# A block's left rows in one tile: per-step loads of 8 rows replaced by a shifted read of zero-padded probabilities

## The chip, the cores and the metric

The kernel runs on one core of one Trainium2 chip. The metric is the device time of one execution in microseconds (us). Engines: PE is TensorE, with PEld for its weight loads; DVE is VectorE, ACT is ScalarE, POOL is GpSimd, SP is SyncE, which here only issues DMAs. Each engine works through its own instructions in program order; a DMA instruction hands a transfer to the 16 DMA engines and lands later.

## The reference, cut to what matters

The output is x + A(xn) + B(xn), with xn the normalised x (2048 rows of 512), and all gradients of it for a given grad_out. B is a two-layer network with a squared ReLU. A is attention with a recurrent memory, 32 heads of 128:

```python
for s in range(n_seg):                          # 64 segments of 32 rows
    xs = x[:, s * seg_len:(s + 1) * seg_len, :].copy()
    h = jnp.concatenate([mem, xs], axis=1)      # 8 memory rows + 32 rows
    q, k, v = (jnp.einsum('btd,dhe->bhte', h, W) for W in (Wq, Wk, Wv))
    scores = jnp.where(mask, jnp.einsum('bhqe,bhke->bhqk', q, k) * scale, -1e9)
    p = _softmax(scores, axis=-1)
    o = jnp.einsum('bhqk,bhke->bhqe', p, v)
    o = jnp.einsum('bhte,hed->btd', o, Wo)
    mem = o[:, :M, :].copy()                    # M = 8: the next segment's memory
```

(q, k, v are three lines in the original.) Each segment needs the memory that the one before it left, so the forward pass is a chain of 64 steps; the gradient is a chain of 64 steps in the other direction.

## The kernel before, in words

**Stages.** From the start to about 255 us of the span: normalisation, B and its gradients, and products that don't depend on the chain. 255 to 1125 us: the forward chain. 1125 to 1385: gradients that don't depend on the backward chain, mixed with weight gradients of B. 1385 to 2335: the backward chain. 2335 to the end: weight gradients of A.

**Main rows and left rows.** Of a step's 40 rows, 32 are its main rows: 8 memory rows and the last 24 of the segment. The first 8 rows of the segment are its left rows; their q, k and v don't depend on the chain and are computed ahead, for many segments at once, and kept in the DRAM tensor S_NL. Four steps make a block (index b, step j = 0 to 3 in it; the backward chain runs j = 3 first and j = 0 last), and a block has 4 x 8 = 32 left rows. Heads are held as 4 groups g of 8 heads k, group g on partitions 32g to 32g+31. The left rows' own attention is done per block (functions left and lback); a main step (functions fwd and bwd) needs the left rows only as 8 further keys, besides its 32 main rows, so it works on L = 40 columns in this order: main 0 to 31, left 32 to 39.

**A forward step** (fwd, line 866): projections of k, q, v; transposes; scores s0, s1 (two halves p of the heads); softmax (mx, sb, ex, su, rc, pm) into the tile E of 64 columns per head, of which the last 24 stay zero; tu (line 480), a DVE transpose of E in 32 x 32 blocks into ET, so that block 0 has the main keys on partitions and block 1 the left keys, on the first 8 of them; w (line 931), the product of probabilities and v by the helper outer (line 620): for each head a matmul over the 32 main rows, and one over the 8 rows of the tile f_vLs; then the output projection.

**f_vLs and b_kLs.** f_vLs holds a step's 8 left rows of v, at partitions 32g to 32g+7, loaded for each step by left_of_step (line 639), four DMAs of 16 KB on SP. In the backward chain b_kLs holds the 8 left rows of k in the same way; there is one buffer of it, so its load for the next step waits until the last product that reads it is done. VL, a block's 32 left rows of v, is loaded besides for the left rows' own attention (line 746).

**A backward step** (bwd, line 1311): o0mm, o1mm, the projection of the incoming gradient (line 422); scores; d1 to d4, the gradient of the scores into gS (line 579); tu, its transposition into gST; vp, kp, qp (helper outer), the gradients of v, k and q, in PSUM tiles, where kp and qp of one half p lie in the same banks; the evictions ve, vl, ke, kl, qe into G4 and others (vea is the first of v; keb0 the first of k); vg, kg, qg, the projections back (line 490); ra, rb, ta, tb, H, the sum that is the next step's input. qp is, for each head, a matmul over the 32 rows of b_kN and one over the 8 rows of b_kLs; qp1, the second half, is the last reader of both. G4 holds a block's main gradients of v, k, q; when the block's last step is done, they are stored to S_GB (line 1238) in six DMAs of 512 KB on SP, named vo1, vo0, qo0, ko0, ko1, qo1. The first step of the next block writes its evictions into the same G4, so these wait for the stores.

**What sets the order.** Two strings written out by hand, F_ORDER and B_ORDER, name every operation in the order in which all engines are given it; each engine's instructions follow that order. A string has four parts, one for each step of a block; a name with n plus signs belongs to the step or block n later or earlier; names with L. are the per-block work. In B_ORDER before, the load of b_kLs is `ldk`, once per step; at the change of blocks SP's order is L.lq (load of b_gqL), vo1, L.qst (a store to S_GL), vo0, qo0, ko0, ko1, ldk, qo1, the load b_vl. POOL issues the loads b_P, b_qN, b_kN and others.

Of the kernel before, what the change touches and what calls it, by code (L numbers as in the profile page):

```python
# [8 lines left out]
ALU = mybir.AluOpType  # L9
# [3 lines left out]
P = 128  # L13
# [13 lines left out]
def kernel(  # L27
# [145 lines left out]
    def masks(pool, temp):  # L173
# [11 lines left out]
        for g in range(HG):  # L185
            sl = slice(32 * g, 32 * g + 32)

            keep(maskA[sl, :, M:SEG], [[0, KM], [-1, XS]], -M, 1)
            nc.gpsimd.memset(maskA[32 * g:32 * g + M, :, :], 0.0)

            keep(maskl1[sl, 0], [[-M, SPB], [0, M]], 0, 1)
            keep(maskl1[sl, 0], [[M, SPB], [0, M]], M - 1, -1)
            keep(maskl1[sl, 1], [[-M, SPB], [-1, M]], 0, 1)
            keep(maskl1[sl, 1], [[-M, SPB], [0, M]], 0, 1)
            keep(maskl1[sl, 1], [[M, SPB], [0, M]], M - 1, -1)
# [298 lines left out]

    C01, C23 = slice(0, 2), slice(2, 4)
# [67 lines left out]
    def ds_ops(o, p, n, sc, Pb, gS, sm):  # L563
# [14 lines left out]
        def d4():  # L578
            nc.vector.scalar_tensor_tensor(out=gS()[:, HALF[p], 0:n], in0=t[0][:], scalar=scale,  # L579
                                           in1=Pb()[:, HALF[p], :], op0=ALU.mult, op1=ALU.mult)  # L580
# [30 lines left out]
    def outer(pp, h, jobs, base=0):  # L611

        for k in range(4):
            for i, (c0, w, ends, m, N_, X) in enumerate(jobs):
                for g in range(HG):
                    o = pp[g // 2][:, g % 2, base + k * c0:base + k * c0 + w]
                    if ends:
                        o = o.rearrange("p (a n) -> p a n", a=2)[:, :, 0:M]
# [16 lines left out]

    def left_of_step(eng, dst, b, j, t):

        for g in range(HG):
            eng(dst[32 * g:32 * g + M], S_NL[b, 32 * g + M * j:32 * g + M * j + M, t, :])
# [14 lines left out]
    def play(order, n, steps, lefts, step, blk, done=None):  # L654
# [25 lines left out]
        "ta+++ Ha+++ L.u2 L.mx0+ L.t1 soV+++ tb+++ L.X2 Hb+++",  # L680
# [5 lines left out]
        "rb+++ L.oa0+ ta+++ Ha+++ tb+++ Hb+++",  # L686
# [4 lines left out]
        "tu1+++ w1+++ L.lq++ oa1+++ ob1+++ g0+++ g1+++ soN++ ra+++ rb+++ ta+++ Ha+++ tb+++ L.otr+ Hb+++",  # L691
# [4 lines left out]
        "ta+++ Ha+++ rb+++ tb+++ Hb+++ km+++ L.t3+ q0mm++++ L.E5+ k0mm++++ L.ra+ xa+++ k0ev++++ q1mm++++ k1mm++++ "  # L696
# [5 lines left out]
    with psum("fr", 4) as fr, psum("fpp", 1) as fpp, \  # L702
# [18 lines left out]
        def block(b):  # L721

            if b not in blk:
# [4 lines left out]
                          "VL": (fo, [P, GW], BF16), "vM": (fo, [P, GW], BF16), "EL": (fo, [P, KH, KW], BF16),  # L728
# [11 lines left out]
        def left(b):  # L740
# [5 lines left out]
            o["lv"] = lambda: dma(B_["VL"][:], S_NL[b][:, 2, :])  # L746
# [28 lines left out]
            for p in range(2):  # L775
                def S_(p=p):
                    ps["s%d" % p] = big("ps_scL")
                    scores(ps["s%d" % p], B_["qL"], ((B_["kM"], NL), (B_["kL"], NL)), p, maskL)
# [8 lines left out]
                def W_(p=p):  # L787
                    ps["w", p] = pair_of_banks()
                    outer(ps["w", p], p, ((32, 32, False, 32, B_["vM"], lambda k: st["ET%d" % p][:, k % 4, 0, :]),
                                          (32, 32, False, 32, B_["VL"], lambda k: st["ET%d" % p][:, k % 4, 1, :])))  # L790
# [75 lines left out]
        def fwd(s):  # L866
# [11 lines left out]
            def load(s1):  # L878

                b1, j1 = divmod(s1, SPB)  # L880
                t = fs.tile([P, GW], BF16, name="f_vLs", tag="vLs")
                left_of_step(dma, t[:], b1, j1, 2)
                vLs[s1] = t

            def ld():
                if s + 1 < NSEG:
                    load(s + 1)
            o["ld"] = ld

            def ld0():  # L890
                turned_rows(B_["kL"][:], 0, 1)
                load(0)
            o["ld0"] = ld0
            o["kl"] = lambda: nc.gpsimd.tensor_copy(T["kT"][:, :, :, SEG:L], B_["kL"][:, :, :, lc])
            o["km"] = lambda: nc.gpsimd.tensor_copy(B_["kM"][:, :, :, lc], T["kT"][:, :, :, 0:M])  # L895

            for t, u, n in ((1, 2, "k"), (0, 1, "q"), (2, 0, "v")):
                for p in range(2):
# [14 lines left out]
                    def Te(n=n, p=p):  # L913
                        ENGS["%s%dTe" % (n, p)](T[n + "T"][:, HALF[p], :, 0:SEG], kgr(ps[n, p]))
                    o["%s%dfl" % (n, p)] = fl_
                    o["%s%dTe" % (n, p)] = Te
            for p in range(2):
# [6 lines left out]
                def tu(p=p):  # L924
                    st["ET%d" % p] = fo.tile([P, 4, 2, 32], BF16, name="ET", tag="ET%d" % p)
                    turn(st["ET%d" % p], E, p)
# [34 lines left out]
        vLs = {}  # L961
# [27 lines left out]
    with sb("la", 2) as la, sb("ls", 2) as ls, sb("lo", 1) as lo_, sb("wg", 2) as wg, psum("lpp", 1) as lpp, psum("lr", 4) as lr:  # L989
# [9 lines left out]
        def lback(i_):  # L999
# [27 lines left out]
            for p in range(2):  # L1027
# [12 lines left out]
                def S_(p=p):  # L1040
                    ps["s", p] = big("ps_sc")
                    scores(ps["s", p], T["gOT"], ((T["vTM"], NL), (T["vTL"], NL)), p, None)
# [8 lines left out]
                def qp(p=p):  # L1051
                    ps["x", p] = [lpp.tile([P, 2, 512], F32, name="l_pp", tag="pp%d" % x) for x in range(2)]
                    outer(ps["x", p], p, ((32, 32, False, 32, T["kM"], lambda k: st[p][:, k % 4, 0, :]),
                                          (32, 32, False, 32, T["kL"], lambda k: st[p][:, k % 4, 1, :])))
# [623 lines left out]
```

## Time and profile before

| what | value |
|---|---|
| median of 3 runs | 2922.25 us (2919.82 to 2928.49) |
| the profiled execution | 2915.0 us |
| its span, first to last instruction | 2913.1 us |
| busy share of the span: PE, PEld, DVE, ACT, POOL | 93%, 50%, 44%, 34%, 23% |
| mean granted TensorE clock | 0.971 |
| DMA packets, bytes | 835429, 561.50 MB |
| loads f_vLs and b_kLs | 256 each, 16 KB each, on SP |
| SP's issue of one of them (min, median, max) | f_vLs 271, 300, 1311 ns; b_kLs 272, 296, 2118 ns |

How to read it: a row of a group is the code line, the engine, the operation, output<-input with partitions x elements, and the count; after the first bar the busy time in us and the mean duration of one in ns; after the second bar the idle time of that engine just before such instructions and what ended it. Four matmuls on four groups of 32 partitions run side by side, so the busy time of a group can be far below count times mean. "issue" is time in which the engine waited for nothing that the profile shows. A granted clock of 0.50 means that TensorE ran at half speed.

### The profile page before, as it was taken

The page shows a single profiled execution, that of the slowest core. Times are in us where ns is not written, and L with a number is a line of the kernel's source. Part 1 is how long each engine was busy: PE and PEld are TensorE (multiplying, and loading weights), DVE is VectorE, ACT ScalarE, POOL GpSimd, SP SyncE. Part 2 cuts the span into 40 slices and gives each one's busy share as a digit, 9 for nine tenths or more (in the row PEclk, how much of TensorE's full clock was granted, in tenths as well). Part 3 has the DMA queues.
Part 4 walks back from the last instruction along what each step waited for, and adds up shares of the span by engine and source line. Part 5 has one row for each costly group of instructions (what it writes and reads, how often), then busy time and mean ns, then how long its engine had stood idle before and what let it go on. Part 6 is the DMA issues. An engine that isn't in the chain of part 4 may idle for free.

```text
span 2913.1 us, 115280 instructions
## 1 busy us (share of the span) xinstructions
PE 2702.2 (93%) x51252; PEld 1450.9 (50%) x51252; DVE 1277.8 (44%) x3754; ACT 1001.7 (34%) x2330; POOL 660.6 (23%) x1278
## 2 busy tenths in 40 slices
PE   7997999999999887888898999999999999999999
PEld 3444555555555555355454554455555444444444
DVE  4533566666665654343454545454445401100000
ACT  2313444444444445232333333333333301111111
POOL 1000000000000001122333433343334324332221
PEclk9998999999999998998899999999999999999999
DMA  9766477667676668999666687677767799999993
GB/s 250 259 207 164 138 184 189 184 188 182 180 192 166 170 156 201 227 225 213 148 167 164 179 220 173 172 180 211 184 170 181 223 273 224 220 209 237 217 210 71
DMA packets 835429, 561.50 MB, mean 193 GB/s; under 512 B 642177, under 2 KB 727698, under 8 KB 833394
## 3 DMA queue, kind: packets, MB, share of 16 engines
q1 hardware_dynamic: 794018, 431.40, 64.6%
q0 software_dynamic: 40912, 122.73, 14.0%
q8 instruction: 402, 6.59, 0.9%
q14 instruction: 97, 0.79, 0.1%
HBM read 174.47 MB, written 234.11 MB: 140 GB/s over the span
## 4 chain that ended last, share of the span: by engine, by line
PE 42%; DMA 7%; issue 2%; DVE 1%; SPq 1%; POOL 0%; ACT 0%; ACTq 0%; DVEq 0%; POOLq 0%
PE ps_gw L1639 17%; PE ps_gR L490 11%; PE ps_proj L422 3%; PE b_pp L620 3%; PE ps_RL L1251 3%; DMA b_kLs<-S_NL 2%; PE b_T L525 1%; PE ps_tr L164 1%; DMA gn<-S_OL 1%; DMA b_qN<-S_A 1%; PE ps_R L490 1%; DMA S_GM<-b_GN 1%; PE b_pp L1383 1%; PE ps_sc L467 1%; DMA b_GN<-GT 0%
## 5 line engine op out<-in xcount | busy, mean ns | idle before, releaser
L1639 PE MATMUL ps_gw<-gn,HNc 128*128 128x512 bf16 x1920 | 416.8, 379 | 0.0
L1639 PEld LDWEIGHTS <-HNc 128*128 128x128 bf16 x1920 | 187.9, 98 | 223.6
L404 ACT CAST f_N<-ps_proj 128x512 bf16<-128x512 f32 x320 | 183.9, 581 | 199.4 <-PE ps_proj L422 192.6
L1572 ACT CAST wt<-ps_gw 128x512 bf16<-128x512 f32 x128 | 74.0, 588 | 451.3 <-PE ps_gw L1639 412.0
L422 PEld LDWEIGHTS <-X 128*32 128x32 bf16 x6144 | 152.6, 96 | 143.1 <-DVE X L534 21.9
L1555 DVE TENSOR_TENSOR gx<-ps_rows,gb 128x512 f32<-128x512 f32 x16 | 11.1, 692 | 426.4 <-PE ps_rows L1553 426.4
L895 POOL COPY kM<-f_kT 128x256 bf16<-128x256 bf16 x64 | 25.8, 403 | 736.0 <-DVE f_kT L407 562.2
L490 PE MATMUL ps_gR<-Wv,gv 128*32 128x512 bf16 x2048 | 145.0, 404 | 6.9 <-issue 6.9
L1639 PE MATMUL ps_gw<-GOc,gn 128*128 128x512 bf16 x640 | 141.0, 383 | 10.2 <-ACT wt L1572 8.7
L490 PE MATMUL ps_gR<-Wk,gk 128*32 128x512 bf16 (+1 forms) x2048 | 141.1, 387 | 1.3 <-ACT gk L404 0.8
L490 PE MATMUL ps_R<-Wo,OT 128*32 128x256 bf16 x4096 | 135.6, 289 | 1.1 <-DVE OT L407 1.1
L422 PE MATMUL ps_proj<-Wq,X 128*32 128x512 bf16 x2048 | 134.7, 380 | 0.1
L404 ACT CAST gk<-b_pp 128x256 bf16<-128x256 f32 x192 | 70.7, 379 | 184.0 <-PE b_pp L620 116.1
L422 PE MATMUL ps_proj<-Wk,X 128*32 128x512 bf16 x2048 | 130.9, 380 | 0.8
L422 PE MATMUL ps_proj<-Wv,X 128*32 128x512 bf16 x2048 | 131.3, 382 | 0.0
L404 ACT CAST gON<-ps_proj 128x512 bf16<-128x512 f32 x128 | 75.0, 586 | 157.4 <-PE ps_proj L422 157.4
L490 PE MATMUL ps_gR<-Wq,gq 128*32 128x512 bf16 (+1 forms) x2048 | 122.8, 348 | 6.8 <-issue 6.8
L422 PE MATMUL ps_proj<-Wo,GT 128*32 128x512 bf16 x2048 | 123.3, 382 | 3.7 <-DVE GT L1296 3.6
L1573 POOL DMA_DIRECT2D out_dram<-wt x120 | 65.0, 543 | 255.7 <-ACT wt L1572 241.0
L1332 POOL COPY PD<-b_P 32x320 bf16<-32x320 bf16 x256 | 115.3, 450 | 8.0
L490 PEld LDWEIGHTS <-OT 128*32 128x32 bf16 x4096 | 109.3, 102 | 9.9 <-DVE OT L407 1.3
L1327 POOL DMA_DIRECT2D b_P<-S_A x63 | 33.9, 538 | 349.9 <-DVE gS L579 115.6
(276 smaller groups left out, 5256.7 us busy)
## 6 DMA issues: line engine op xcount, KB each, us to landing
S_A<-f_N SPq DMA_DIRECT2D x64, 512.0 KB
out_dram<-wt POOLq DMA_DIRECT2D x134, 128.0 KB, 4.9
S_A<-f_N SPq DMA_DIRECT2D x64, 256.0 KB
S_GB<-gv SPq DMA_DIRECT2D x32, 512.0 KB
S_GB<-gq SPq DMA_DIRECT2D x32, 512.0 KB
S_GB<-gk SPq DMA_DIRECT2D x32, 512.0 KB
b_kN<-S_A POOLq DMA_DIRECT2D x63, 256.0 KB, 3.9
b_qN<-S_A POOLq DMA_DIRECT2D x63, 256.0 KB, 4.1
```

What stands on the lines that cost most here:

```text
L164: nc.tensor.transpose(ps_ap, in_ap, ident[base:base + k, base:base + k])
L404: nc.scalar.copy(out, in_)
L422: nc.tensor.matmul(o, lhsT=hT[:, dc, :], rhs=x, start=(dc == 0), stop=(dc == DC - 1), tile_position=(0, 32 * g))
L467: nc.tensor.matmul(sc3[32 * g:32 * g + 32, k, c:c + n], lhsT=qT[:, 4 * h + k, g, :], rhs=kT[:, 4 * h + k, g, :], start=(mask is None), sto ...
L490: nc.tensor.matmul(R[32 * g:32 * g + 32, 0:(cs.stop - cs.start) * P].rearrange("p (a b) -> p a b", b=P), lhsT=XT(k, g), rhs=x[:, cs, :], s ...
L620: nc.tensor.matmul(o, lhsT=N_[32 * g:32 * g + m, kk * P:(kk + 1) * P], rhs=X(kk)[32 * g:32 * g + m], start=(i == 0), stop=(i == len(jobs) ...
L1251: nc.tensor.matmul(ps["R", i][32 * g:32 * g + 32, :].rearrange("p (a b) -> p a b", b=P), lhsT=B_[n][:, k, g, :], rhs=W(g * KH + k), start= ...
L1327: q(tile_of("P", [P, KH, KW])[:], rows[:, 3 * GW:AC].rearrange("p (k n) -> p k n", k=KH))
L1332: nc.gpsimd.tensor_copy(PD[32 * g:32 * g + 32, g], C["P"][32 * g:32 * g + 32, :, 0:L])
L1572: nc.scalar.copy(wt[:], ps[:])
L1573: eng(dst, wt[:])
L1639: nc.tensor.matmul(ps[:], lhsT=l(rc), rhs=r(rc), start=(n == 0), stop=(n == RC_ALL - 1))
```

## The change

In both chains a step's columns are put in the order left 0 to 7, main 8 to 39, and the 40 columns stand at the right end of the 64 of E and gS: columns 0 to 23 are zero, 24 to 31 left, 32 to 63 main. The DVE transpose then reads two windows of 32 columns per head: one from column 24 - 8j on, one from column 32 on. In the first window of step j the 8 left columns land on partitions 8j to 8j+7, behind 8j zeros; the product over it takes the first 8 + 8j rows of a tile that holds all left rows of the block, VL forward and kNL backward, so that the rows of other steps meet zeros. left_of_step, f_vLs and b_kLs are gone.

The forward chain uses VL, which now has two buffers and is loaded at the end of the first part of F_ORDER, one part earlier than before. The backward chain loads kNL once per block, in two halves (ldk1, then ldk0, 128 KB each) into one buffer; in SP's order these come right behind the first projections of the block's first step: ldk1, vo1, L.qst, ldk0, vo0, qo0, ko0, ko1, qo1. The rest of B_ORDER and F_ORDER names the same operations in the same order as before; the cuts between the four parts of B_ORDER lie elsewhere. Masks, copies and evictions take the columns at their new places.

```diff
-    def turn(ET, E, h):
-        nc.vector.transpose(ET[:].rearrange("p k a q -> p (k a q)"),
-                            E[:, HALF[h], :].rearrange("p k n -> p (k n)"))
+    def turn(ET, E, h, j=None):
+        if j is None:
...
+        else:
+            x = E[:, HALF[h], XS - M * j:]
+            nc.vector.transpose(ET[:].rearrange("p k a q -> p (k a q)"),
+                                bass.AP(x.tensor, x.offset, [x.ap[0], [KW, 4], [M + M * j, 2], [1, SEG]]))
...
-            e.tensor_tensor(out=E()[:, HALF[p], 0:n], in0=st[p][:], in1=bc(ss[1], n), op=ALU.mult)
+            e.tensor_tensor(out=E()[:, HALF[p], KW - n:KW], in0=st[p][:], in1=bc(ss[1], n), op=ALU.mult)
...
-    def left_of_step(eng, dst, b, j, t):
-        for g in range(HG):
-            eng(dst[32 * g:32 * g + M], S_NL[b, 32 * g + M * j:32 * g + M * j + M, t, :])
...
-                          "VL": (fo, [P, GW], BF16), "vM": (fo, [P, GW], BF16), "EL": (fo, [P, KH, KW], BF16),
+                          "VL": (fs, [P, GW], BF16), "vM": (fo, [P, GW], BF16), "EL": (fo, [P, KH, KW], BF16),
...
-                    outer(ps["w", p], p, ((32, 32, False, 32, T["N"][:, 0], lambda k: st["ET%d" % p][:, k % 4, 0, :]),
-                                          (32, 32, False, M, vLs[s], lambda k: st["ET%d" % p][:, k % 4, 1, :])))
+                    outer(ps["w", p], p, ((32, 32, False, 32, T["N"][:, 0], lambda k: st["ET%d" % p][:, k % 4, 1, :]),
+                                          (32, 32, False, M + M * j, B_["VL"], lambda k: st["ET%d" % p][:, k % 4, 0, :])))
...
-        "o0mm++++ pb+++ o1mm++++ L.vo1+ L.qst o0ev++++ L.vo0+ xa+++ L.xt L.qo0+ o1ev++++ o0fl++++ xb+++ L.ra0+ "
+        "o0mm++++ pb+++ o1mm++++ ldk1+++ L.vo1+ L.qst o0ev++++ ldk0+++ L.vo0+ xa+++ L.xt L.qo0+ o1ev++++ o0fl++++ "
...
-            o["ldk"] = lambda: left_of_step(dma, tile_of("kLs", [P, GW])[:], b, j, 1)
+            for p in range(2):
+                o["ldk%d" % p] = lambda p=p: dma(B_["kNL"][:, HC[p]], S_NL[b][:, 1, HC[p]]) if j == SPB - 1 else None
...
-                                     (32, 32, False, M, C["kLs"], lambda k: st[p][:, k % 4, 1, :])), 4 * KW)
+                                     (32, 32, False, M + M * j, B_["kNL"], lambda k: st[p][:, k % 4, 0, :])), 4 * KW)
```

More of the change, by code (lines that the diff above doesn't have):

```diff
@@ L493, in gather @@
                                  tile_position=(0, 32 * g))
+    MAIN = slice(M, L)
     C01, C23 = slice(0, 2), slice(2, 4)
@@ L578, in d4 @@
         def d4():
-            nc.vector.scalar_tensor_tensor(out=gS()[:, HALF[p], 0:n], in0=t[0][:], scalar=scale,
+            nc.vector.scalar_tensor_tensor(out=gS()[:, HALF[p], KW - n:KW], in0=t[0][:], scalar=scale,
                                            in1=Pb()[:, HALF[p], :], op0=ALU.mult, op1=ALU.mult)
@@ L745, in left @@
             o["lq"] = lambda: turned_rows(B_["qL"][:], b, 0)
-            o["lv"] = lambda: dma(B_["VL"][:], S_NL[b][:, 2, :])
+            o["lv"] = lambda: dma(B_["VL"][:], S_NL[b][:, 2, :]) if b > 0 else None
             o["lm"] = lambda: memory_rows(B_["vM"], b, 0)
@@ L876, in fwd @@
             ps, st, o = {}, {}, {}
[L878 to L888, printed above, removed]
             def ld0():
                 turned_rows(B_["kL"][:], 0, 1)
-                load(0)
+                dma(B_["VL"][:], S_NL[0][:, 2, :])
             o["ld0"] = ld0
-            o["kl"] = lambda: nc.gpsimd.tensor_copy(T["kT"][:, :, :, SEG:L], B_["kL"][:, :, :, lc])
-            o["km"] = lambda: nc.gpsimd.tensor_copy(B_["kM"][:, :, :, lc], T["kT"][:, :, :, 0:M])
+            o["kl"] = lambda: nc.gpsimd.tensor_copy(T["kT"][:, :, :, 0:M], B_["kL"][:, :, :, lc])
+            o["km"] = lambda: nc.gpsimd.tensor_copy(B_["kM"][:, :, :, lc], T["kT"][:, :, :, M:2 * M])
             for t, u, n in ((1, 2, "k"), (0, 1, "q"), (2, 0, "v")):
@@ L913, in Te @@
                     def Te(n=n, p=p):
-                        ENGS["%s%dTe" % (n, p)](T[n + "T"][:, HALF[p], :, 0:SEG], kgr(ps[n, p]))
+                        ENGS["%s%dTe" % (n, p)](T[n + "T"][:, HALF[p], :, MAIN if n == "k" else slice(0, SEG)], kgr(ps[n, p]))
                     o["%s%dfl" % (n, p)] = fl_
@@ L1384, in vp @@
                                          start=True, stop=False, skip_group_check=True)
-                        nc.tensor.matmul(o.rearrange("p g (a n) -> p g a n", a=2)[:, :, :, 0:M],
+                        nc.tensor.matmul(o[:, :, 0:2 * M].rearrange("p g (a n) -> p g a n", a=2),
                                          lhsT=B_["gOL"][:, k * P:(k + 1) * P],
@@ L1411, in bwd @@
                         o[e] = lambda n=n, x=x, gs=gs, p=p, at=at, w=w, e=e: ENGS[e](
-                            G4[n][:, gs, HALF[p], j, :], two_of(pp(p), x, w, *at)[:, :, :, 0:SEG])
+                            G4[n][:, gs, HALF[p], j, :], two_of(pp(p), x, w, *at)[:, :, :, MAIN if n == "k" else slice(0, SEG)])
                         if n == "k":
@@ L1471 @@
             first["ldn"](dma)
-            first["ldk"]()
+            first["ldk0"]()
+            first["ldk1"]()
             ldk(NB - 1, dma)
             for s in range(1, NSEG):
-                for n in ("vtr", "vc", "ldp", "pb", "ldq", "ldn", "ldk"):
+                for n in ("vtr", "vc", "ldp", "pb", "ldq", "ldn", "ldk0", "ldk1"):
                     steps[NSEG - s][n] = steps[NSEG - 1 - s][n]
-            for n in ("vtr", "vc", "ldp", "pb", "ldq", "ldn", "ldk"):
+            for n in ("vtr", "vc", "ldp", "pb", "ldq", "ldn", "ldk0", "ldk1"):
                 steps[0][n] = lambda: None
```

68 lines of the change are left out of this document (34 added, 34 removed), and 61 rows, old and new, of tables (B_ORDER, F_ORDER).

## The prediction

> **What bounds the kernel now.** I read the busy time by stage first, then who waits for whom in the backward recurrence, then the groups by shape, then the timelines of block ends. The first view cuts the span at the stage borders; its columns are the time, the busy us of PE, PEld, DVE, ACT and POOL, the granted clock, the DMA share and GB/s. The two chains that the change touches:
>
> ```profile
> 255.00:1125.00 870.00, 819.35 (x20735) 476.66 (x20734) 537.54 (x1686) 413.61 (x937) 55.58 (x135) 0.97 0.66 173
> 1385.00:2335.00 950.00, 875.48 (x22824) 474.85 (x22822) 462.77 (x1452) 359.57 (x977) 362.89 (x700) 0.97 0.72 184
> ```
>
> TensorE is busy 94% and 92% of them, so only what stops TensorE, or slows its clock, is worth time: 51 us forward and 75 us backward stand idle. The second view lists PE's waits in the backward chain (us in total, times, longest):
>
> ```profile
> PE b_pp L620 <- issue: 14.7, 9, 2.5
> PE b_pp L620 <- DMA b_kLs<-S_NL: 14.5, 16, 4.8
> PE ps_gR L490 <- issue: 13.9, 10, 3.0
> PE b_pp L620 <- ACT gk L404: 6.0, 5, 1.6
> PE b_pp L620 <- DMA b_qN<-S_A: 4.8, 7, 1.0
> ```
>
> The load that the change removes, b_kLs, is the largest wait with a name. In the chain that ended last it has 2.1% (61 us), but that counts the load's whole time; PE stood for 14.5 us of it. The forward twin f_vLs is in no PE wait (PEld waited 2.5 us for it), and the forward waits are for ET (24.0 us).
>
> **What the removed waits are worth.** From the PE timeline I measured each backward step from its first projection matmul to that of the next. A block's four steps, in the order they run: first 17.0 us (mean of 15 blocks, 14.8 to 19.4), second and third about 13.1 and 12.7 in every block, last 15.9 (14.05 to 20.8). So all that can be won lies in the first and the last step. In the last step b_kLs is late where SP, which issues in order, stood behind a chain of transposes:
>
> ```profile
> 1546.63 0.20 PE L620 MATMUL b_pp<-gST,b_kN 32*128 32x32 bf16 x4
> 1551.60 0.91 PE L620 MATMUL b_pp<-gST,b_kLs 8*128 8x32 bf16 x4 [4.77 <-DMA b_kLs<-S_NL]
> ```
>
> PE stops 4.77 us between two halves of one product. Such waits in last steps are 4.77, 0.61, 0.30, 1.32, 0.59, 0.71, 1.49 and 0.99: 10.8 us. The six steps that have them took 20.8, 16.7, 14.15, 17.9, 18.0 and 15.6 us, where the five undisturbed ones took 14.05 to 14.3: 18.5 us over 14.1 each. The 7.7 us beyond the idle time are slow clock: it reads 0.50 from 1549 to 1555. After the change nothing of this block is loaded in the last step, so I count **-18.5 us**. The Trainium skill (TensorE: Matmul & The Clock Gate, What's actually happening) has the clock halve only after an idle window of about 3.4 us; by that only the 4.77 us wait costs clock and this term would be about -13. The rows differ: after 0.68, 1.65 and 0.66 us of waiting between 1978 and 1983 the clock was 0.50 until 1989. I keep the rows.
>
> In the first step the waits with b_kLs's name are only 0.35, 0.66, 0.58 and 1.13 us, and there something else ends as late. SP's timeline of one block end, then what ACT and PE waited for (idle time and releaser in brackets):
>
> ```profile
> 1966.24 0.35 SPq L1216 DMA_DIRECT2D b_gqL<-S_GQL  x1
> 1966.70 1.95 SPq L1238 DMA_DIRECT2D S_GB<-gv  x1
> 1968.69 0.42 SPq L1283 DMA_DIRECT2D S_GL<-gNat  x1
> 1969.17 1.15 SPq L1238 DMA_DIRECT2D S_GB<-gv  x1
> 1970.41 0.91 SPq L1238 DMA_DIRECT2D S_GB<-gq  x1
> 1971.37 3.45 SPq L1238 DMA_DIRECT2D S_GB<-gk  x2
> 1974.86 4.17 SPq L639 DMA_DIRECT2D b_kLs<-S_NL  x4
> ...
> 1981.66 0.37 ACT L404 CAST gk<-b_pp 128x256 bf16<-128x256 f32 x1 [2.73 <-DMA S_GB<-gk]
> ...
> 1982.94 0.81 PE L620 MATMUL b_pp<-gST,b_kLs 8*128 8x32 bf16 x4 [0.66 <-DMA b_kLs<-S_NL]
> ```
>
> Six stores of 512 KB go out; from 1970 to 1982 the 16 DMA engines are full (share about 1.0, 300 to 400 GB/s). The next step's gk eviction waits for the first gk store to have left G4, qp0 waits for that eviction (they share a PSUM bank), and b_kLs, queued behind all stores, lands 1 us later. Both end late together.
>
> **What the change moves there.** The block's kNL (two halves of 128 KB, one buffer) is loaded ahead of vo1 and vo0, the gv stores. Its buffer is read by qp1 of the block's last step, so SP now stands at ldk1 until that is done. Call its last matmul group's start Q: 1911.21, 1968.24, 2204.22 in three blocks; vo1 went out before it, at 1910.31, 1966.70, 2202.67. Behind the waiting ldk1 on SP are vo1, the S_GL store, ldk0, vo0, qo0, ko0, ko1. Where the two gv stores go back to back and ACT then waits for ko0, that wait ended 13.2, 13.8 and 14.2 us after vo1 (three blocks). New vo1: Q + 0.2 + 0.45 (one issue). ko0 has then landed at about Q + 0.65 + 13.7 = Q + 14.4; in the eight blocks where ACT waited for it, it ended 12.9 after Q on average. PE's first kLs group now comes 13.9 us after Q (mean of 15); then Q + 14.4 + 0.45 = 14.85: +0.95 a block, +14 us over 15. In the same stretch PE now stands some 20 us for "issue" (2.85 at 1567.23, 2.55 at 1803.51), which the longer wait partly covers; I take a quarter of that off: **+9.5 us**. kNL's 256 KB against the 64 KB of b_kLs would add 0.5 us a block at 380 GB/s, but the 256 KB b_gqL load, first of the burst today, goes 1 to 2 us earlier once the four b_kLs issues ahead of it are gone (1.3 to 1.7 us of SP); I set these equal.
>
> **Parts that cost nothing.**
>
> ```profile
> L620 PE MATMUL b_pp<-gST,b_kLs 8*128 8x32 bf16 x2048 | 54.5, 175 | 22.5 <-DMA b_kLs<-S_NL 14.5 <-issue 7.3
> L620 PE MATMUL b_pp<-gST,b_kN 32*128 32x32 bf16 x2048 | 51.8, 177 | 7.9 <-ACT gk L404 6.0 <-issue 1.4 <-ACT b_gkL L404 0.4
> L620 PEld LDWEIGHTS <-b_kLs 8*128 8x128 bf16 x2048 | 39.3, 92 | 27.4 <-DMA b_kLs<-S_NL 16.2 <-issue 7.8
> L620 PEld LDWEIGHTS <-b_kN 32*128 32x128 bf16 x2048 | 37.8, 91 | 48.3 <-issue 46.8 <-DMA b_kN<-S_A 1.3
> ```
>
> The contraction over 8, 16, 24 or 32 rows in place of 8: 8 rows take 175 and 92 ns, 32 rows 177 and 91. No cost, and the count stays. Forward, 256 loads of 16 KB (1.2 us of SP a step) go, and the block's VL comes up to a step earlier, in two buffers; PE waited for neither, so 0; if a VL is late, w0 waits, at most what b_kLs cost in last steps. At blocks 4, 8 and 12 VL is read right after the store of its last rows; w0 is more than half a step later and covers it. STREAM_TRANSPOSE (445 and 440 ns) reads four overlapping windows instead of 256 contiguous columns: no row shows that. Nearest are reductions: 344 ns for 192 strided elements, 299 for 160 contiguous, the same per element, so I take 0; below nothing is excluded, the count of elements is the same. If it doubled, the 26 forward waits for ET and 6 backward ones for gS would pay 0.44 each: +14. The moved columns in masks, copies and evictions keep shapes and counts: 0.
>
> **Sum.** -18.5 + 9.5 = -9 us on the profiled execution's 2915.0 (span 2913.1, 1.9 around it): 2906. The median of the runs shown is 7.25 above that execution: **2913 us**. About 0.3% (9 us) is what a measurement of this kernel can tell from no change.
>
> **Rivals.**
> *The gain stays whole.* Across the 15 first steps the time from Q to kLs does not follow how early vo0 went (14.0 or so for early and late ones), which speaks for a burst that may shift free of charge. Then -18.5, -2.7 for the waits in first steps, and up to -10 of "issue" as the burst meets a stopped PE: -21 to -31, 2891 to 2901.
> *The stores become the wait (slower).* ldk1 delays vo0 from Q - 1.0 (mean of 15) to Q + 2.2. Counted from vo0, ko0 landed 12.75 us later (mean of eight); with 0.5 us for kNL that is Q + 15.5, PE at Q + 15.9, +2 a block: +30. The three blocks whose vo0 went after Q have first steps of 17.65, 19.4 and 18.9 us against a mean of 17.0, which speaks for it. With slow clock after the longer waits (1.5 us in half of the blocks) +41; less 18.5: +11 to +23, 2933 to 2945. It decides from 1.2 us a block on (18.5/15). The Trainium skill (DMA: Bandwidth & Descriptors, Queues, rings and completion order) says that an engine takes descriptors in ring order, so what stands ahead of ko0 is moved first; the trace shows SP's stores landing so, b_kLs after ko0.
> *The shifted read is slow:* +14 on the sum, 2927.
> *b_kLs was never the end of a wait:* "issue" gaps fill it, 0, 2922.
>
> **Chances.** Forecast 0.42 (its own range 2900 to 2924: faster 0.24, same 0.18), whole gain 0.16 (faster), stores 0.30 (slower 0.28, same 0.02), slow read 0.05 (slower 0.04, same 0.01), nothing 0.07 (same 0.05, slower 0.02). Together faster 0.40, same 0.26, slower 0.34. The range takes the whole gain's far end and the stores with all their slow clock and 10 us of first-step waits more: 2891 to 2955.
>
> **What would show it.** Last steps of blocks all at 14.1 to 14.5 us: the -18.5. Time from Q to the first kNL group near 14.9, with ACT waiting for S_GB<-gk in nearly all blocks: the +9.5; at 16, the stores rival; at 13.9 or less, the whole gain. STREAM_TRANSPOSE near 445 ns and a forward stage of 870 us: the zeros. The prediction is wrong if the waits for VL or kNL themselves appear on PE, or if the forward stage moves by more than 5 us.

## The result and the profile after

The changed kernel takes 2932.07 us (median of 20 runs, 2915.5 to 2946.9) where the kernel before takes 2916.52 us (20 runs, 2898.5 to 2933.75): the ratio is 1.0057, 95% interval 1.0039 to 1.0075. In a second comparison it was 1.0073 (1.0040 to 1.0107). The range of the prediction holds the time, but the sign is wrong: 9 us faster was forecast and it is 16 to 20 us slower. Most runs of a kernel lie within 20 us of its median, single ones 30 us away, and the kernel before is at 2901.6 to 2907.9 us in the later comparisons. So below a kernel is compared only with the kernel before of the same comparison: by the ratio with its 95% interval, or by the difference of the two medians in us.

The profiled execution took 2933.0 us (span 2931.2). First the two chains by stage, in the columns of the view shown of before (time, busy us of PE, PEld, DVE, ACT, POOL, clock, DMA share, GB/s), then the five longest of PE's waits in the backward chain (us in total, times, longest; 1385 to 2355 us, since the chain ends later than before):

```profile
255.00:1125.00 870.00, 807.71 (x20632) 468.90 (x20674) 535.55 (x1681) 408.54 (x930) 55.59 (x135) 0.98 0.65 168
1385.00:2335.00 950.00, 864.39 (x22566) 467.01 (x22569) 455.65 (x1435) 355.30 (x968) 359.61 (x698) 0.96 0.73 177
```

```profile
PE b_pp L626 <- ACT b_gvL L404: 16.7, 7, 3.3
PE ps_gR L495 <- issue: 10.5, 13, 2.4
PE b_pp L1372 <- DMA b_gOL<-S_GOL: 10.0, 5, 4.6
PE b_pp L626 <- ACT gk L404: 8.3, 8, 1.6
PE b_pp L626 <- DMA b_qN<-S_A: 7.2, 4, 2.7
```

PE is busy 91% of the backward stage instead of 92%. The wait for b_kLs is gone, and no wait for b_kNL has come. In its place stand waits for the v evictions, for b_gOL and for b_qN, which were small or absent. All of those for the v evictions (b_gvL) and for b_gOL are in the first step of a block. One block end, SP first, then the two ACT evictions and the PE groups that waited (idle time and releaser in brackets):

```profile
2216.86 0.33 SPq L1202 DMA_DIRECT2D b_gqL<-S_GQL  x1
2217.86 0.33 SPq L1323 DMA_DIRECT2D b_kNL<-S_NL  x1
2218.24 1.07 SPq L1224 DMA_DIRECT2D S_GB<-gv  x1
2219.36 0.44 SPq L1269 DMA_DIRECT2D S_GL<-gNat  x1
2219.85 0.81 SPq L1323 DMA_DIRECT2D b_kNL<-S_NL  x1
2220.70 1.13 SPq L1224 DMA_DIRECT2D S_GB<-gv  x1
2221.93 0.56 SPq L1224 DMA_DIRECT2D S_GB<-gq  x1
2222.53 2.86 SPq L1224 DMA_DIRECT2D S_GB<-gk  x2
2225.48 1.90 SPq L1224 DMA_DIRECT2D S_GB<-gq  x1
2227.48 6.03 SPq L1327 DMA_TRANSPOSE b_vl<-S_A  x1
...
2229.31 0.59 ACT L404 CAST gv<-b_pp 128x512 bf16<-128x512 f32 x1 [3.91 <-DMA S_GB<-gv]
2233.34 0.37 ACT L404 CAST gk<-b_pp 128x256 bf16<-128x256 f32 x1 [2.62 <-DMA S_GB<-gk]
...
2230.60 0.38 PE L626 MATMUL b_pp<-gS,b_qN 32*128 32x40 bf16 x4 [2.70 <-DMA b_qN<-S_A]
2233.76 0.21 PE L626 MATMUL b_pp<-gST,b_kN 32*128 32x32 bf16 x2 [0.62 <-ACT gk L404]
```

Q is 2217.53 here. The first kNL load leaves right after it, as forecast, and all six stores behind it. ACT now waits for a gk store in 15 of 15 blocks (33.4 us; 8 blocks and 19.9 us before) and, which nothing forecast, for a gv store in 9 (33.5 us; 4 and 3.5 us before). Two more things are to be seen, and the runs below turn on them: no issue stands between the second gk store and the second gq store, where before had four (4.17 us in the block that the prediction shows), and b_vl follows at once.

The rows for the parts that were to cost nothing:

```profile
L485 DVE STREAM_TRANSPOSE ET<-E 128x256 bf16<-128x256 bf16 x128 | 57.0, 445 | 4.4
L485 DVE STREAM_TRANSPOSE gST<-gS 128x256 bf16<-128x256 bf16 x128 | 56.3, 440 | 2.2
L626 PE MATMUL b_pp<-gST,b_kNL 8*128 8x32 bf16 x512 | 11.9, 172 | 1.0 <-issue 0.8
L626 PE MATMUL b_pp<-gST,b_kNL 32*128 32x32 bf16 x512 | 11.2, 177 | 0.0
```

The backward steps, from the timelines (mean us; a step runs from its first gON eviction to that of the next). "gq" and "vl" say how long after the first gk store the second gq store and the load of b_vl left SP (mean of 15 blocks). Each row is one execution; the backward chain of the kernel before took 933.1 us in one and 924.4 in another, so a row tells 0.3 us a step at best.

| kernel | first | second | third | last | gq | vl |
|---|---|---|---|---|---|---|
| before | 16.98 | 13.12 | 13.12 | 15.90 | 8.1 | 9.0 |
| before, second execution | 17.08 | 13.06 | 13.05 | 15.43 | 8.0 | 8.9 |
| changed | 19.56 | 13.10 | 12.94 | 14.33 | 3.3 | 5.5 |
| changed, second execution | 18.99 | 13.05 | 12.87 | 14.19 | 3.0 | 4.8 |

Read alone, these traces say: 1.6 and 1.2 us won in each last step, 2.6 and 1.9 lost in each first one, the stores' rival as it was described. The runs show that this is not the whole of it.

### The profile page after: what moved, and what is told of

Same layout as the page of the kernel before. It is cut to its first block, busy times and chain, and to the rows that moved or that the text cites. A ratio compares the mean times of both kernels' runs of the same rounds, so it can differ in the third digit from the quotient of the medians.

```text
span 2931.2 us, 114549 instructions
## 1 busy us (share of the span) xinstructions
PE 2691.9 (92%) x51115; PEld 1444.8 (49%) x51252; DVE 1276.8 (44%) x3754; ACT 1002.0 (34%) x2330; POOL 659.3 (22%) x1278
## 3 DMA queue, kind: packets, MB, share of 16 engines
q0 software_dynamic: 40912, 122.73, 14.3%
q8 instruction: 402, 6.59, 1.0%
## 4 chain that ended last, share of the span: by engine, by line
PE 71%; DMA 13%; SPq 6%; DVE 4%; issue 3%; ACT 2%; POOL 1%; another core or an unknown queue 0%; ACTq 0%; DVEq 0%; POOLq 0%
PE ps_gw L1627 15%; PE ps_proj L422 14%; PE ps_gR L495 11%; PE ps_R L495 4%; DMA S_GB<-gk 3%; PE b_pp L626 3%; PE ps_tr L164 3%; PE ps_RL L1237 2%; SPq L1072 2%; PE ps_L L380 2%; PE ps_sc L467 2%; PE ps_B L341 2%; PE f_T L531 2%; PE f_pp L626 2%; PE ps_gxb L350 1%
## 5 line engine op out<-in xcount | busy, mean ns | idle before, releaser
L495 PE MATMUL ps_gR<-Wv,gv 128*32 128x512 bf16 x2048 | 151.8, 419 | 1.3 <-issue 1.2
L495 PE MATMUL ps_R<-Wo,OT 128*32 128x256 bf16 x4096 | 128.1, 279 | 1.1 <-DVE OT L407 1.1
```

The source lines that it names most:

```text
L495: nc.tensor.matmul(R[32 * g:32 * g + 32, 0:(cs.stop - cs.start) * P].rearrange("p (a b) -> p a b", b=P), lhsT=XT(k, g), rhs=x[:, cs, :], s ...
```

## Experiments

**1. The order, the place, the forward half.** Theory W was the rival of the prediction: SP stands at the kNL load, so all stores leave later. Theory V blames the bytes of that load, theory U the shifted reads, the deeper contraction or the moved columns.

*order_only*: the kernel before with `ldk+++` taken from behind `L.ko1+` and put ahead of `L.vo1+`.

> The kernel before, with one edit: the load of the step's 8 left rows of k (64 KB, b_kLs) goes to the place in the order that the change gives kNL, ahead of the stores of the finished block, in all first steps of a block; tiles, shifted reads and the loads of the other steps are as before. Theory W (SP stands at the load until the block's last query product has started its last group, and all six stores leave later): first store about 2.8 us later than before (from Q - 2.1 to Q + 0.7), first kLs group from Q + 13.7 to Q + 15.7, first steps of blocks from 17.0 to about 19.5 us, so +30 to +39 us: 2946 to 2955 beside 2916.5. Theory V (the bytes ahead of the stores, not the wait): only 64 KB go ahead, 0.2 us a block, at most +3 us: 2920. Theory U (the shifted reads, the deeper contraction or the moved columns): nothing of them is in this kernel: 2916.5.

Measured 1.0063 (1.0039 to 1.0087), 14.6 us more. First steps 17.87, last 15.01. The first store leaves even later than in the changed kernel (at Q + 1.7 against Q + 0.9; Q - 2.7 before), but first steps lengthen by 0.9 us, not by 2.5, and the first kLs group starts at Q + 14.1, not at Q + 15.7.

*late*: the changed kernel with `ldk1+++ ldk0+++` behind `L.ko1+`.

> The changed kernel, with one edit: the two 128 KB loads of kNL go behind the stores, to the place where the 64 KB load of b_kLs stood before (after the second gk store); still one buffer. Theory W: the first store leaves at about Q - 2 again, the wait of the gk eviction for its store ends at Q + 13 or earlier, first steps 17.0 to 17.7 us and last steps stay at 14.3: 24 us less in last steps and 0 to 10 us more in first steps than the kernel before, 2895 to 2909 (up to 6 us more if the forward chain's +6.4 us is real). Theory V: the 256 KB now land behind the last gk store, 0.5 to 0.7 us later than the 64 KB did, so PE waits for b_kNL in most first steps, up to 18.4 us: 2909 to 2917. Theory U: the order does nothing, first steps stay at 19.6: 2932.

Measured 1.0061 (1.0039 to 1.0084), first steps 17.74, last steps 15.07. The stores leave as early as before and nothing is won: W and V both miss, by 18 us and more. The total is what U expects, the first steps are not (19.6).

*fwd_only*: before with the forward half of the change.

> The kernel before with the forward half of the change alone (VL in one tile of two buffers, shifted read of the probabilities, order of the forward chain); its backward chain is the one of before and so reads the probabilities' columns in the old places, which hold other columns now: its gradients are not the reference's, its instructions and shapes are those of before. If the forward chain's +6.4 us in the changed kernel's trace is of the change: forward 850 us, 2922 to 2923. If it is chance (one step of 17.5 us in which ACT and PE stood for nothing that the profile shows): 844 to 846, 2916.5, within 3 us. No theory expects a change of its backward steps (first 17.0, last 15.9).

Measured 1.0013 (0.9992 to 1.0034). The forward half costs nothing that can be measured. From the first eviction into R to the last the forward chain took 844.5 us in the kernel before, 850.7 and 841.2 in two executions of the changed one, and 841.4 here.

*half3*: kNL in two half tiles with `bufs=3`, first half loaded at the start of the last step, second half still ahead of the stores; b_GN in gNat's buffer.

> The changed kernel, with kNL as two half tiles (128 KB each) that rotate through three buffers: the first half of the next block is loaded at the start of the block's last step, the second half at the changed kernel's place ahead of the stores, where its buffer has been free since the last step's first query product; to make room b_GN shares the buffer of gNat, so its transposing load waits for the store of gNat on SP in the third step. Theory W: no wait on SP ahead of the stores, first store at Q - 2 or earlier, first steps 16.5 to 17.2 us, no kNL wait, last steps 14.3: 2885 to 2900 (up to 6 us more if the forward chain's +6.4 us is real). Theory V: 128 KB still go ahead of the stores, half of the changed kernel's extra time stays: first steps 18.3, 2912. Theory U: 2932. If sharing b_GN's buffer costs, the third steps are longer than 12.9 us.

Measured 1.0140 (1.0095 to 1.0185), first steps 20.3. It doesn't test what it was meant to: with b_GN in gNat's buffer SP's transposing loads came later, and in 7 of 15 blocks the first gv store left more than 2 us after Q. It is 34 us slower: late stores go with a loss, but the four issues behind the second gk store are missing here too, so the 34 us are not the stores' alone.

**2. No load at all.** The first entry is the profile of the kernel before that stands in the table.

> The kernel before, profiled on the same chip as the next three, since three kernels so far were timed on a chip where the kernel before takes 2901.6 us and not 2916.5. If the differences of single traces are to be trusted, first steps of a block are 16.9 to 17.0 us and last steps 15.2 to 15.9 here too; if last steps are nearer 15.0, the 24 us that the changed kernel's trace showed in last steps is partly the choice of the execution.

> The changed kernel again, against the kernel before on one chip: all theories expect 0.4% to 0.75% longer, first steps 19 to 20 us, last steps 14.1 to 14.5.

The kernel before took 2904.22 us in that one run, the changed one is at 1.0073 of it (1.0040 to 1.0107). With last steps of before at 15.43 in place of 15.90, about 7 of the 24 us (1.57 in each of 15 last steps) that the first pair of traces showed are the difference between two executions of one kernel.

Theory V2 puts W and V together: the wait at the load and its 256 KB in the stretch of the stores.

*noload*: one kNL tile, `dma(...) if s == NSEG - 1 else None`.

> The changed kernel without the loads of kNL in 15 of its 16 blocks: the first block's kNL is read in all blocks, so the products of the score gradients with the left rows of k (and what follows from them) are not the reference's; all else, the shifted reads and the order too, is as in the changed kernel. Theory V2 (what costs is where the kNL load stands, its wait and its 256 KB in the stretch where the DMA engines are full): first steps back to 16.5 to 17.0, last 14.3, 24 to 32 us less than the kernel before, 0.989 to 0.992 of it. Theory W (the wait alone): the same. Theory U (something else of the change in the backward chain costs, and the load nothing): 1.0057 as the changed kernel.

Measured 1.0047 (1.0019 to 1.0074), and 1.0044 (1.0020 to 1.0068) when it was run again as noload_b. Without any of the loads the changed kernel is still 13 us slower than before. So the wait at the load and its bytes are not the main cause, and W and V2 fall. The total is near what U expects; section 4 tests U.

*half3b*: three half buffers, b_GN in gOT's buffer, `ldk0++++` after `vtr++++` and `ldk1++++` before `L.lq++` in the last step; `L.gst+` goes ahead of `L.gl++`.

> The kernel with three half buffers for kNL, mended: b_GN shares the buffer of gOT, which is free when it is needed, and no longer that of gNat (whose chain of transposing loads made SP 2 to 4 us late at block ends); both halves are loaded within the last step, the first after the load of b_vl, the second ahead of b_gqL's load, so none stands in the stretch of the stores and none waits for the block's last query product. Theory V2 and W: first steps 16.5 to 17.2, last steps 14.1 to 14.6, 15 to 30 us less than the kernel before: 0.990 to 0.995. Theory U: 1.005. If SP is late again (first gv store after Q instead of Q - 2), the kernel does not test this.

Measured 1.0018 (0.9988 to 1.0048): last steps 14.14, as hoped, and first steps 17.88. All kernels so far that lack the four issues behind the second gk store have first steps of 17.7 us or more. (One of them, late, has two loads of 128 KB in that place. There the second gq store leaves 6.6 us after the first gk store and b_vl 8.0, and PE waits 9.4 us for b_kNL in first steps.)

**3. What SP no longer does.** Theory S: the four small issues held SP back while the 16 DMA engines were full.

*before_noldk*: before, `if j == SPB - 1` the load is left out.

> The kernel before without the 64 KB load of b_kLs for the first step of 15 blocks (four issues on SP behind the second gk store); those steps read the left rows of the step before, so the gradients that come from them are not the reference's. Theory S (the four issues, 4.2 to 4.7 us of SP while the rings are full, held back the last gq store of 512 KB and the b_vl load behind it; without them these leave about 4 us earlier, into the stretch where the stores and POOL's loads already fill the DMA engines): work is left out and the kernel gets slower, first steps from 17.0 to 17.8, 5 to 13 us more than the kernel before, with PE waiting for b_qN or for its instructions in their place. Rival: the load only cost what PE waited for it there (4.6 us in the last trace): 3 to 6 us less than the kernel before.

Measured 1.0030 (1.0010 to 1.0051): a load is left out and it is 10 us slower. The total is as S says; the first steps of its trace are not (17.01).

*before_qo1*: before with `L.qo1+` ahead of `ldk+++`.

> The kernel before with one store moved: the second gq store goes out right behind the second gk store, ahead of the four issues of b_kLs. Theory S: the store competes with the loads on POOL's queue 4 us earlier, and b_kLs for the first step lands behind it, first steps from 17.0 to 18 or more: 10 to 20 us more than the kernel before. Rival (order within SP's queue behind the gk stores does not matter, only what is ahead of them): b_kLs 1.5 us later in the blocks where PE waits for it, 3 to 8 us more, and no more waiting for b_qN.

Measured 1.0068 (1.0042 to 1.0094), as much as the whole change, by moving one store. The waits of PE in its backward chain begin with

```profile
PE b_pp L620 <- DMA b_kLs<-S_NL: 35.3, 25, 4.7
```

so here the store mainly makes the loads behind it late, as the rival has it, at S's price.

*half3b_qlate* and *half3b_kfirst* reorder the stores of half3b (`L.qo1+` after `vtr++++`; `L.ko0+` ahead of `L.qo0+`).

> The kernel with three half buffers and both halves of kNL loaded in the last step (first steps 17.9, last 14.15 in its trace), with the second gq store moved behind the load of b_vl. Theory S: the store leaves 1.3 to 6 us later, the waits for b_qN and for instructions in first steps get shorter, 17.9 to about 17.2: 5 to 12 us less than that kernel, 0.995 to 0.999 of the kernel before. Rival: the first steps are bound by the first gk store (11.4 us of waits for the gk eviction): no change, 1.0005 to 1.003.

> The same kernel with three half buffers, with the first gk store moved ahead of the first gq store, nothing else. If first steps are bound by the landing of the first gk store (PE waited 11.4 us for gk evictions in its trace), it lands 1.3 to 1.5 us earlier, the wait ends that much earlier or passes to the gq eviction: up to 15 us less than without, 0.995 to 0.998 of the kernel before. If something else ends as late (b_qN, instructions, theory S): no change, 1.0005 to 1.003.

Measured 1.0003 (0.9983 to 1.0023) and 0.9996 (0.9971 to 1.0022), first steps 18.08 and 17.77. Neither can be told from half3b or from before; S expected first steps of 17.2 in half3b_qlate. There gq leaves 9.4 us after the first gk store, later than in the kernel before (8.1), but b_vl at 3.2: only one of the two is held back, and the first steps stay long. In before_qo1 it is the other one (gq 3.4, b_vl 10.0), and they are long too (18.14).

**4. Each term by itself.** Theory G: what a last step gains is given back in the next first step. *before_nolast* leaves out the load of the last step (`if j == 0`), *before_nokls* all but the first (`if s < NSEG - 1`), *noload_four* adds four loads of 16 KB (`ld4+++`) behind `L.ko1+` in noload_b.

> The kernel before without the load of b_kLs for the last step of each block (those steps read the left rows of the step before, so the gradients that come from them are not the reference's); nothing else is changed. The step of the prediction that is tested: the waits of the last step are worth 18.5 us. If that holds, the time is 14 to 19 us less than the kernel before, 0.9935 to 0.995. Theory G (given back: the stores of the block leave on a schedule that SP's chain of transposing loads sets, so a last step that ends earlier only makes the next first step wait longer for them): last steps 14.2, first steps from 17.0 to 17.7 or 17.9, sum of the two from 32.5 to about 32.0: 5 to 8 us less at most, 0.997 to 0.9985, and no gain at all if DMA work also moves into the stretch of the stores.

> The kernel before without the loads of b_kLs in all steps but the very first (all steps read those rows, so the gradients from the left rows are not the reference's); old reads, old order. Theory G with S: little or nothing won, 0.998 to 1.004, although 63 loads are gone. Prediction's step: 18.5 us from last steps and 4 to 5 from first steps, 0.992. Theory U (the shifted reads, the deeper contraction or the moved columns cost in the changed kernel): this kernel is clearly faster than noload_b beside it, by 10 us or more.

> The changed kernel without the loads of kNL in 15 of 16 blocks (the first block's rows are read in all blocks, so the gradients from the left rows of k are not the reference's), again, beside the two others on one chip. It differs from before_nokls only in the shifted reads, the moved columns, the deeper contraction and the forward chain. Theories G and S: equal to before_nokls within 6 us. Theory U: 10 us or more slower than it.

> noload_b with four loads of 16 KB put back behind the second gk store, as the kernel before has them there (they overwrite rows of the one kNL tile, whose values are not the reference's in any case). Theory S (the four issues hold back the last gq store and the b_vl load while the DMA engines are full): more work and less time, 4 to 10 us less than noload_b, first steps 17.0 to 17.4. Rival: the products wait for the rows that land behind the stores: 2 to 6 us more than noload_b.

| kernel | ratio to before (95%) | first | last |
|---|---|---|---|
| before_nolast | 0.9978 (0.9960 to 0.9996) | 17.15 | 14.75 |
| before_nokls | 1.0032 (1.0014 to 1.0050) | 17.97 | 14.56 |
| noload_b | 1.0044 (1.0020 to 1.0068) | 17.94 | 14.42 |
| noload_four | 1.0003 (0.9981 to 1.0026) | 17.20 | 14.84 |

Three answers. The load of the last step is worth 5.6 us (interval 1 to 12), not 18.5: the total is what G expects, the first steps (17.15) are not the 17.7 to 17.9 of G. before_nokls and noload_b are 3 us apart, so the shifted reads, the deeper contraction and the moved columns cost nothing that these runs can tell, and theory U, which needs 10 us, falls. And noload_four does more than noload_b and is 13.4 us faster by the medians (by the means of 12 runs each 12.0, 95% interval 4 to 20). SP of noload_b and of noload_four at one block end:

```profile
2187.49 0.43 SPq L1225 DMA_DIRECT2D S_GB<-gv  x1
2187.97 0.43 SPq L1270 DMA_DIRECT2D S_GL<-gNat  x1
2188.45 1.08 SPq L1225 DMA_DIRECT2D S_GB<-gv  x1
2189.62 0.57 SPq L1225 DMA_DIRECT2D S_GB<-gq  x1
2190.24 3.65 SPq L1225 DMA_DIRECT2D S_GB<-gk  x2
2193.93 1.84 SPq L1225 DMA_DIRECT2D S_GB<-gq  x1
2195.88 5.44 SPq L1328 DMA_TRANSPOSE b_vl<-S_A  x1
```

```profile
2187.09 3.52 SPq L1229 DMA_DIRECT2D S_GB<-gk  x2
2190.65 5.42 SPq L635 DMA_DIRECT2D b_kNL<-S_NL  x4
2196.51 0.56 SPq L1229 DMA_DIRECT2D S_GB<-gq  x1
2197.17 1.81 SPq L1333 DMA_TRANSPOSE b_vl<-S_A  x1
```

Four issues of 16 KB take 5.42 us here. Behind them the second gq store (512 KB) leaves 9.4 us after the gk stores began and takes 0.56 us to issue; without them it leaves 3.7 us after and takes 1.84, and b_vl's transposing load stands 5.44 us on SP where it takes 1.81 in the other. In the mean of 15 blocks gq leaves at 8.2 against 3.2 us and b_vl at 9.0 against 5.3. The Trainium skill (DMA: Bandwidth & Descriptors, Rules for kernel authors) says to coalesce many small transfers into one, since under 64 KB one pays mostly overhead. Here the four transfers of 16 KB held SP for 5.42 us in the block shown, and the kernel that has them is the faster one all the same. That the time on SP is what helps is argued from these timelines; no run holds SP back without transfers.

**5. Kernels that compute all of the reference.** *before_ldkfirst* moves the last step's `ldk+++` ahead of `L.ldt++`; *half3b_four* is half3b with four loads of 8 KB behind `L.ko1+`.

> The kernel before with one move: the load of b_kLs for the last step goes ahead of the transposing loads of b_vTL and b_vl on SP; all of the reference is computed. If the 5.6 us that before_nolast won (0.9978) came from the lateness of that load alone, this gets most of it: 2 to 7 us less than the kernel before, 0.9975 to 0.9993. Rival: the transposing loads, each 1 to 2 us later behind it, make the chain of SP, and so the stores, later: 0 to 6 us more.

> The changed kernel with kNL in three half buffers, loaded in the last step, and with four loads of 8 KB behind the second gk store (8 rows of each group of the second half are loaded again, with the same values); all of the reference is computed. Without the four loads it was at 1.0018 (0.9988 to 1.0048). Theory S, from noload_four against noload_b (13.4 us less): 0.996 to 0.9985. If the second half's last products wait for the rows that land behind the stores, as b_kLs did in some first steps, 2 to 5 us of it are lost again. Rival (the four issues help only where the first gk store is not what PE waits for): no change, 1.000 to 1.003.

before_ldkfirst: 1.0009 (0.9983 to 1.0034). Its last steps are 14.29 and its first steps 18.04, though the four issues stand behind the gk stores as before (gq 8.5, b_vl 9.5): the shorter last steps win nothing in the total. half3b_four: 0.9974 (0.9948 to 1.0000), with first steps of 17.23 and last steps of 14.32. The changed form is about 5 us faster than the kernel before, median to median, when its load stands outside the stretch of the stores and SP is held back there as before; the interval reaches 1.0000, so even this gain is barely clear of none. Against half3b, in another comparison, the four loads make 0.0044 by the ratios, 12.8 us, but only 2.9 us by the medians, each taken against the kernel before; this pair alone would not carry theory S.

## Why the prediction was wrong, point by point

- **-18.5 us for the last steps: this step failed.** The waits did go, and the last steps came to 14.3 and 14.2 us. But the sum took all that six last steps had over 14.1 us as the load's doing and as won. Taken away alone (before_nolast), the load was worth 5.6 us. Where the rest stayed is shown in part.

  Other waits come forward: in the trace of before_nolast no last step waits for b_kLs, and still only ten of 15 are short (mean 14.05); the other five take 15.25 to 18.05 us, with PE standing 0.67 to 2.23 us for "issue" in each.

  And a shorter last step can make the next first step longer, as in before_ldkfirst, because the stores don't leave as much earlier. In the trace of before the first gv store leaves 5.7 us after the start of the last step in the six blocks with a last step under 14.6 us and 7.6 us after it in the nine others, 1.9 us apart where the last steps are 2.94 us apart (14.14 and 17.08). It stands on SP behind the load of b_gqL, which waits for the transposing load of that tile and leaves at 5.1 and 7.2 us. The first steps that follow are 17.87 and 16.40 us, so half of the 2.94 us is given back there; in the second execution it is 1.1 of 2.2 us, but in the trace of fwd_only, with the same backward instructions, 0.2 of 2.8. How much is given back therefore stays open; that the sum of both steps has to be priced, and not the last step, is what the prediction left out.

  The reading of this term by the Trainium skill (TensorE: Matmul & The Clock Gate, What's actually happening), in which only the longest wait costs clock, gave an estimate of about 13 us; that is more than the run showed as well, so this case does not decide between the two.
- **+9.5 us for the kNL load ahead of the stores.** Its place was right, and ACT did wait for a gk store, in 15 and 14 of 15 blocks of the two executions. Q to the first kNL group took 15.7 us, and 15.1 in the second execution (13.7 and 13.3 before): 2.0 and 1.8 us a block, where 0.95 was forecast and the stores' rival said 2. The 13.7 us from the first gv store to the landed gk store came from three blocks whose gv stores left 0.9 us apart. In the changed kernel ldk0 stands between them and they leave 2.2 us apart; the five other blocks of before, with 1.8 to 3.3 us between, have 13.9 to 15.7 us, 15.0 in the mean. And lateness of the stores alone does less: in order_only the first gv store left at Q + 1.7 and the first kLs group started at Q + 14.1, where 13.7 us for the landing would give Q + 15.8. What the load costs by itself is what the changed kernel has over noload: 15.6 and 20.2 us against 13.8 and 13.2, about 4 us, and their intervals overlap, so its size is not settled.
- **The term that was missing: this is what turned the sign.** The prediction saw b_kLs "queued behind all stores", counted its four issues (4.17 us) as something that only makes b_kLs late, and so put their removal at nothing. They also held back the second gq store and the load of b_vl, by 5 and 4 us, while the 16 DMA engines were full. Taking them away costs 13.4 us (noload_b against noload_four), 15.6 us (before_nokls against before_nolast, which differ in other loads too), 10.0 us (before_noldk) and 12.8 or 2.9 us (half3b against half3b_four, by ratios or by medians). The times carry this more than the traces do. In three of the four pairs the first steps differ by 0.65 to 0.8 us, 10 to 12 us over 15 blocks, but their last steps differ the other way by 0.2 to 0.4 us; before_noldk's first steps (17.01) don't show it at all. And of the two executions profiled, noload_four's was the longer (2908.8 against 2904.1 us).
- **The sum, by the runs:** -5.6 (last step's load) + 13.4 (issues gone) + 4 (load ahead of the stores) = +12, where 15.6 and 20.2 were measured. The rest is within what the intervals leave open. That the range holds the time is in the main luck: its upper part was drawn for late stores, and most of the loss has another source.
- **The zeros held:** shifted read 445 and 440 ns, contraction over 8 rows 172 ns and over 32 rows 177 ns, forward 1.0013, no wait of PE for VL or kNL. The prediction's sign that the forward stage moves by more than 5 us did come in the first trace (6.2 us longer); the second (3.3 us shorter) and fwd_only show it to be the execution's, not the change's.
- **The rivals.** The stores' rival (2933 to 2945) gave the right sign, and 16 to 20 us is in its +11 to +23. Its reason is about a quarter of it by the medians: late has early stores and is as slow, noload has them and is 13 to 14 us slower than before. No rival had a load that helps by being in the way.
- **Open:** whether the gq store and the b_vl load do the harm only together (with one of them held back alone, in half3b_qlate and before_qo1, the first steps stayed long), and through which of PE's waits. Late isn't explained either: its two loads held SP back for most of that time, and it is as slow as the changed kernel. In noload_b and noload_four the waits with names differ little (b_qN 11.0 against 7.5 us); waits for "issue" make 45.2 and 38.4 us between 1385 and 2310 us.

## What to carry to other kernels

A wait that goes away is worth what is left after other waits have come forward and the next step has answered: price the sum of both steps, in more than one execution. Before small DMAs are taken off an in-order queue that also carries large stores, ask what follows them there: they may be what holds the next transfers back while the DMA engines are full. And test a removal by leaving the work out: if the kernel gets slower without it, it was holding something back.

## What was not expected of the hardware

- Issuing took long where the DMA engines were full (share 1.03 to 1.07 in the stretches shown): in the kernel before, four loads of 16 KB held SP 3.1 to 5.7 us behind the gk stores (median of 15 blocks 4.65), against a median of 1.33 us elsewhere, and the transposing loads shown held it 5.44 and 6.03 us against a median of 1.31.
- The page of the profile lists a DMA queue of the kind "instruction" with 6.59 MB in 402 packets in the run, beside a hardware_dynamic queue whose packets take 64% of the engines' time; PE stood for "issue" in every kernel here, up to 4.3 us at a time in the backward chain, and at other places in each execution. That the one makes the other wasn't tried.
